# The last token tile of a Conformer kernel: residual on TensorE, two halves of the features, statistics and normalisation from PSUM on two engines, square root on ScalarE

## Chip, cores, metric

One core of one Trainium2 chip. The metric is the device time of one execution in microseconds, median of several. The kernel before takes 2054.47 us (median of 3 runs, 2052.74 to 2055.17), so a tail of a few microseconds is all that this change can touch.

## The reference

A Conformer block in bf16: x is 2 x 4000 tokens of 512 features. The last step is what matters here: half of the second feed-forward's result is added to x3, and the sum is normalised over the 512 features of each token.

```python
def _layernorm(x, axis=-1, eps=1e-05):
    m = jnp.mean(x, axis=axis, keepdims=True)
    v = jnp.var(x, axis=axis, keepdims=True)
    return (x - m) / jnp.sqrt(v + eps)
...
    h = _layernorm(x3, axis=-1)
    h = _silu(h @ w_ff2_a) @ w_ff2_b        # 512 -> 2048 -> 512
    x4 = x3 + 0.5 * h
    return _layernorm(x4, axis=-1)
```

## The kernel before

Tokens are worked in chunks of four tiles of 127 tokens; the last chunk has three. `ff_last` is the second feed-forward of that last chunk and the last work of the kernel. For each tile it accumulates 16 matmuls of 512 columns in one PSUM bank, then VectorE adds the residual, takes mean and variance, GpSimd takes the power -1/2, VectorE normalises, and two queues (SP 112 rows, ACT 15 rows) store.

```python
    def ff_last(self, c, old):
        ...                                        # 16 blocks of the first matmul and Silu
        sl = self.nxt("ln", self.LN_SLOTS)
        for ti in range(token_tiles(c)):
            for f in range(FC):
                self.ff_second(f, ti, *blocks[f], f == FC - 1)
            self.residual(self.Yb[ti][0:TILE, :], self.b_Y[ti], c * TPC + ti, 0.5)
            self.ln_stats(c, sl, ti)               # DVE bn_stats from SBUF
            self.ln_mean(sl, ti)                   # DVE bn_aggr
            self.ln_factor(sl, ti)                 # DVE add eps, POOL pow -0.5
            self.ln_norm(c, sl, ti, self.osb[0][:, ti, :], self.b_osb[0][ti], "DVE")
            self.store_out(c, self.osb[0], self.b_osb[0], ti, ti + 1, ("SP", "ACT"))

    def residual(self, ps, b_ps, g, scalar, b_scalar=(), rows=slice(0, TILE)):
        self.S.op("DVE", lambda e: e.scalar_tensor_tensor(
            out=self.XT[g][rows], in0=ps[rows], scalar=scalar, in1=self.XT[g][rows], op0=ALU.mult, op1=ALU.add),
            reads=[b_ps, self.bx[g]] + list(b_scalar), writes=[self.bx[g]])
```

Two other places come into the argument. The program ends with a branch that every engine takes past a second program (a fallback that this input does not need), and the place where the attention loop starts pieces of the convolution:

```python
    def build(self):
        ...
        self.program(False)
        fits = nc.values_load(self.flag, ...)
        self.wait_out()
        with nc.If(fits < 1):                      # the fallback program
            S.barrier()
            self.program(True)
            self.wait_out()
...
        def att_hook(g, kt):
            ...
            if kt in (22, 27) and (0 <= g - 1 < tail or g - 1 == tail and (22, 27).index(kt) < self.KEEP):
                pair(g - 1, (22, 27).index(kt))    # matmuls on tiles that the SP queue transposes
```

## Time and profile before

| | kernel before |
|---|---|
| time, median of 3 | 2054.47 us |
| span of the profiled run, granted clock | 2047.4 us, 1.000 |
| first matmul of the last tile to the store's issue on SP | 6.63 us |
| of which after the last matmul's end | 3.01 us |
| store's issue to its last landing; to the end of the span | 2.44; 2.63 us |

The last three rows are read from the timeline of the last 10 us and from the store's landings; the prediction below shows the timeline's lines. "Landing" is the moment at which the store's completion reaches the semaphore that SP waits for before it ends; in this profile that is 0.91 us after the packet of the last row has ended (1.52 us after the issue).

The view of the store's own instructions of the kernel before, cut to the last one, gives the landings of its two queues (us from issue):

```profile
DMA to landing us min/median/max: 1.9/2.2/2.4
```

The 15 rows of the ACT queue land after 1.9 us, the 112 rows of SP after 2.4.

### The profile page before, as it was taken

The numbers are of one execution on the slowest core, as the hardware profiler recorded it, in microseconds if no ns is written. First come the engines' busy times: TensorE is split into PE (matmuls) and PEld (weight loads), VectorE is DVE, ScalarE is ACT, GpSimd is POOL, SyncE is SP. The second block draws the span as 40 slices with busy tenths as digits, with TensorE's granted clock in tenths as the row PEclk, the third lists the DMA queues.
The fourth block names the chain that finished last, engine by engine and source line by source line (L and its number), as shares of the span: only waits on it lengthen the run. The fifth ranks groups of instructions, "written<-read, shape, count | busy, mean of one in ns | idle before, by whom it ended". The sixth has DMA issues, their size and how long they took to land.

```text
span 2047.4 us, 24513 instructions
## 1 busy us (share of the span) xinstructions
PE 2029.9 (99%) x9647; PEld 1028.7 (50%) x9649; DVE 1092.7 (53%) x2264; ACT 744.9 (36%) x1274; POOL 109.7 (5%) x236
## 2 busy tenths in 40 slices
PE   9999999999999999999999999999999999999998
PEld 5555555554444444444444444444445555555555
DVE  4244443334556667666766676667674434434434
ACT  3433333333333333333333333333345443433433
POOL 1000000000000000000000000000011000000000
PEclk9999999999999999999999999999999999999999
DMA  8222245420101011104411111011143111111111
GB/s 182 54 62 62 53 100 125 96 70 8 26 16 31 22 31 26 30 24 108 113 34 23 26 29 32 23 26 29 42 135 93 31 31 42 31 31 42 26 36 38
DMA packets 253120, 104.41 MB, mean 51 GB/s; under 512 B 193412, under 2 KB 252487, under 8 KB 252999
## 3 DMA queue, kind: packets, MB, share of 16 engines
q1 hardware_dynamic: 252751, 102.61, 21.2%
q8 instruction: 78, 1.28, 0.3%
q14 instruction: 43, 0.35, 0.1%
q10 hardware_dynamic: 248, 0.18, 0.0%
HBM read 33.77 MB, written 23.34 MB: 28 GB/s over the span
## 4 chain that ended last, share of the span: by engine, by line
PE 97%; DVE 1%; DMA 0%; SPq 0%; issue 0%; POOL 0%; ACT 0%; POOLq 0%; DVEq 0%; ACTq 0%
PE s L500 55%; PE y L500 42%; DVE wff L1176 0%; SPq L558 0%; DVE work L612 0%; DMA work<-work 0%; DMA wff<-in_w_ff_a_dram 0%; DVE xt L753 0%; SPq L562 0%; DVE work L634 0%; POOL work L726 0%; POOL work L1185 0%; ACT work L550 0%; DVE work L547 0%; SPq L554 0%
## 5 line engine op out<-in xcount | busy, mean ns | idle before, releaser
L550 ACT ACTIVATE work<-s 128x508 bf16<-128x508 f32 (+3 forms) x1060 | 622.8, 588 | 1211.9 <-PE s L500 1208.3
L500 PE MATMUL s<-work,wff 128*128 128x508 bf16 (+5 forms) x2624 | 628.3, 371 | 6.4 <-issue 3.5
L500 PE MATMUL s<-work,keys 128*128 128x508 bf16 (+1 forms) x2048 | 516.8, 374 | 0.1
L500 PE MATMUL y<-work,keys 128*128 128x508 bf16 (+2 forms) x2048 | 504.2, 373 | 0.4 <-DVE work L999 0.4
L500 PE MATMUL y<-wff,work 128*127 128x512 bf16 x1992 | 501.2, 379 | 0.0
L920 DVE TENSOR_TENSOR work<-work 128x508 f32<-128x508 f32 (+2 forms) x496 | 334.5, 674 | 279.8 <-ACT work L550 278.6
L500 PEld LDWEIGHTS s<-work,wff 128*128 128x128 bf16 x2624 | 252.2, 98 | 283.1 <-issue 10.1
L500 PEld LDWEIGHTS y<-wff,work 128*127 128x127 bf16 x1992 | 273.7, 137 | 171.4
L500 PEld LDWEIGHTS s<-work,keys 128*128 128x128 bf16 x2048 | 199.5, 98 | 231.9 <-issue 0.6
L500 PEld LDWEIGHTS y<-work,keys 128*128 128x128 bf16 (+1 forms) x2048 | 193.5, 97 | 234.0 <-issue 6.2
L753 DVE SCALAR_TENSOR_TENSOR xt<-y,xt 127x512 bf16<-127x512 f32 x126 | 78.5, 683 | 360.5 <-PE y L500 360.5
L612 DVE BATCH_NORM_STATS2 work<-xt 127x6 f32<-127x512 bf16 x312 | 197.2, 680 | 5.9 <-DMA xt<-in_x_dram 5.8
L500 PE MATMUL s<-work 128*127 128x512 bf16 (+3 forms) x776 | 197.0, 378 | 2.2 <-DVE work L1292 1.2
L621 POOL TENSOR_TENSOR work<-work 127x4 f32<-127x4 f32 (+1 forms) x76 | 76.7, 1009 | 1133.6 <-DVE work L619 1133.6
L500 PEld LDWEIGHTS s<-work 128*127 128x127 bf16 (+1 forms) x776 | 94.9, 124 | 77.0 <-issue 3.8
L634 DVE TENSOR_SCALAR work<-xt,work 127x512 bf16<-127x512 bf16 x307 | 110.7, 406 | 26.2 <-POOL work L621 23.0
L753 DVE SCALAR_TENSOR_TENSOR xt<-s,xt 127x512 bf16<-127x512 f32 x55 | 38.0, 692 | 144.6 <-PE s L500 144.6
L753 DVE SCALAR_TENSOR_TENSOR xt<-s,work,xt 127x512 bf16<-127x512 f32 x64 | 48.0, 750 | 30.8 <-PE s L500 30.2
L1074 DVE SCALAR_TENSOR_TENSOR wff<-wff,s 128x508 bf16<-128x508 f32 (+1 forms) x57 | 38.7, 678 | 45.3 <-PE s L500 45.1
L550 ACT ACTIVATE wff<-s 128x508 f32<-128x508 f32 (+1 forms) x67 | 39.5, 591 | 58.7 <-PE s L500 58.7
L550 ACT ACTIVATE work<-keys,work 128x508 bf16<-128x508 bf16 (+1 forms) x68 | 52.2, 774 | 1.4 <-DVE work L1190 1.3
L1155 POOL COPY wff<-wff 128x1 bf16<-128x1 bf16 x56 | 10.5, 188 | 638.8 <-DVE wff L1074 636.4
(83 smaller groups left out, 424.0 us busy)
## 6 DMA issues: line engine op xcount, KB each, us to landing
keys<-keysd SPq DMA_DIRECT2D x62, 128.0 KB, 2.3
keysd<-work SPq DMA_DIRECT2D x14, 448.0 KB, 3.2
out_dram<-work SPq DMA_DIRECT2D x14, 448.0 KB, 3.2
dcvd<-wff SPq DMA_DIRECT2D x48, 127.0 KB, 1.8
keys<-dcvd SPq DMA_DIRECT2D x12, 508.0 KB, 5.1
xt<-in_x_dram SPq DMA_DIRECT2D x13, 448.0 KB, 4.9
wff<-in_w_ff_a_dram SPq DMA_DIRECT2D x16, 256.0 KB, 6.3
work<-work SPq DMA_TRANSPOSE x208, 2.5
```

What stands on the lines that cost most here:

```text
L500: self.S.op("PE", lambda e: e.matmul(out, lhsT, rhs, start=start, stop=stop, **kw), reads=reads, writes=[bank], inc=stop if inc is None el ...
L550: return self.S.op("ACT", lambda e: e.activation(out, in_, func, **kw), reads=reads, writes=writes)
L612: self.S.op("DVE", lambda e: e.bn_stats(self.st[sl][:, ti, :], x), reads=[b_x], writes=[self.b_st[sl][ti]])
L621: S.op("POOL", lambda e: e.tensor_tensor(out=self.rs[sl][:, 0:n], in0=self.va[sl][:, 0:n], in1=self.neghalf[0:TILE, 0:n], op=ALU.pow), rea ...
L634: self.S.op("DVE", lambda e: e.tensor_scalar(out, x, self.mv[sl][:, ti, 0:1], self.rs[sl][:, ti:ti + 1], ALU.subtract, ALU.mult), reads=[b ...
L753: self.S.op("DVE", lambda e: e.scalar_tensor_tensor(out=self.XT[g][rows], in0=ps[rows], scalar=scalar, in1=self.XT[g][rows], op0=ALU.mult, ...
L920: S.op("DVE", lambda e, p=p, n=n, acc=acc: e.tensor_tensor(out=acc, in0=acc, in1=self.P[p][0:n, 0:W], op=ALU.add), reads=[self.b_P[p], sel ...
L1074: self.S.op("DVE", lambda e: e.scalar_tensor_tensor(out=out, in0=th, scalar=1.0, in1=ps[:, 0:W], op0=ALU.add, op1=ALU.mult), reads=[b_ps, ...
L1155: S.op("POOL", lambda e: e.tensor_copy(self.G[gs][:, jj, 0:1], self.G[gp][:, jj, CHUNK:CHUNK + 1]), reads=[self.b_G[gp][jj]], writes=[self ...
```

## The change

The intent: shorten the chain behind the last matmul. TensorE, which accumulates anyway, adds 2·x through a matmul with twice the identity (so PSUM holds 2·x3 + h; a layernorm of twice the vector with four times epsilon is the same); the features go in two halves to two banks, so that the first half's statistics run beside the second half's matmuls; the factor comes from ScalarE's square root and a reciprocal; and VectorE and ScalarE normalise one half each straight from PSUM. Setup lines and declarations are cut.

```diff
@@ def ff_last(self, c, old):
+        S.op("DVE", lambda e: e.tensor_scalar(self.two, self.ident, 2.0, None, ALU.mult), ...)
...
-        sl = self.nxt("ln", self.LN_SLOTS)
-        for ti in range(token_tiles(c)):
+        self.act(self.nr1, self.onef, AF.Sqrt, [self.b_onef], [self.b_nr1])     # loads the table early
+        sl, n = self.nxt("ln", self.LN_SLOTS), token_tiles(c)
+        for ti in range(n - 1):
...
+        ti, g = n - 1, c * TPC + n - 1
+        st, b_st = self.st[sl][:, ti:ti + 2, :], self.b_st[sl][ti:ti + 2]
+        halves = [(self.Yb[k], self.b_Y[k], slice(m * D // 2, (m + 1) * D // 2)) for m, k in enumerate((0, ti))]
+        for m, (ps, b_ps, d) in enumerate(halves):
+            self.mm(ps[0:TILE, d], self.two[0:TILE, 0:TILE], self.XT[g][:, d], True, False, [self.b_two, self.bx[g]], b_ps)
+            for f, (p, b_p) in enumerate(blocks):
+                self.mm(ps[0:TILE, d], p[:, ti * TILE:(ti + 1) * TILE], self.Wb[:, f, d], False, f == FC - 1,
+                        [self.b_Wb[f], b_p], b_ps)
+            S.op("DVE", lambda e, m=m, ps=ps, d=d: e.bn_stats(st[:, m, :], ps[0:TILE, d]), reads=[b_ps], writes=[b_st[m]])
+        S.op("DVE", lambda e: e.bn_aggr(self.mv[sl][:, ti, :], st.rearrange("p t s -> p (t s)")), ...)
+        self.act(sd, self.mv[sl][:, ti, 1:2], AF.Sqrt, [...], [b_sd], bias=self.eps4[0:TILE])     # 4 * EPS
+        S.op("DVE", lambda e: e.reciprocal(self.rs[sl][:, ti:ti + 1], sd), ...)
+        S.op("DVE", lambda e: e.scalar_tensor_tensor(out=sh, in0=mean, scalar=-1.0, in1=rs, op0=ALU.mult, op1=ALU.mult), ...)
+        for m, (ps, b_ps, d) in enumerate(halves):
+            if m == 0:
+                S.op("DVE", lambda e, ps=ps, d=d: e.tensor_scalar(o[:, d], ps[0:TILE, d], mean, rs, ALU.subtract, ALU.mult), ...)
+            else:
+                self.act(o[:, d], ps[0:TILE, d], AF.Identity, [...], [b_o[ti + 1]], bias=sh, scale=rs)
+        self.store_out(c, self.osb[0], b_o, ti, ti + 2, ("SP", "ACT"))
```

More of the change, by code (lines that the diff above doesn't have):

```diff
@@ L384, in memory @@
         self.b_late = [A.buf("late", k * 1024, 2 * CHUNK) for k in range(FC - self.NP)]
+        self.two = A.view(60 * 1024, 128)
+        self.b_two = A.buf("two", 60 * 1024, 256)
         ns = self.LN_SLOTS
@@ L412, in memory @@
         self.b_nr1 = Buf("nr1")
+        self.eps4 = small(1)
+        self.b_eps4 = Buf("eps4")
         self.onef = small(1)
@@ L795, in ff_last @@
         S, late = self.S, FC - self.NP
+        S.op("DVE", lambda e: e.tensor_scalar(self.two, self.ident, 2.0, None, ALU.mult), reads=[self.b_ident], writes=[self.b_two])
         blocks = []
@@ L817, in ff_last @@
             self.store_out(c, self.osb[0], self.b_osb[0], ti, ti + 1, ("SP", "ACT"))
+        ti, g = n - 1, c * TPC + n - 1
[7 more added lines that the diff above has]
+            S.op("DVE", lambda e, m=m, ps=ps, d=d: e.bn_stats(st[:, m, :], ps[0:TILE, d]), reads=[b_ps], writes=[b_st[m]])
+        S.op("DVE", lambda e: e.bn_aggr(self.mv[sl][:, ti, :], st.rearrange("p t s -> p (t s)")),
+             reads=b_st, writes=[self.b_mv[sl][ti]])
+        sd, b_sd = self.va[sl][:, ti:ti + 1], self.b_va[sl][ti]
+        self.act(sd, self.mv[sl][:, ti, 1:2], AF.Sqrt, [self.b_mv[sl][ti], self.b_eps4], [b_sd], bias=self.eps4[0:TILE])
+        S.op("DVE", lambda e: e.reciprocal(self.rs[sl][:, ti:ti + 1], sd), reads=[b_sd], writes=[self.b_rs[sl][ti]])
+        o, b_o = self.osb[0][:, ti, :], self.b_osb[0]
+        mean, rs, sh = self.mv[sl][:, ti, 0:1], self.rs[sl][:, ti:ti + 1], self.sh[sl][:, ti:ti + 1]
+        b_mv, b_rs, b_sh = self.b_mv[sl][ti], self.b_rs[sl][ti], self.b_sh[sl][ti]
+        S.op("DVE", lambda e: e.scalar_tensor_tensor(out=sh, in0=mean, scalar=-1.0, in1=rs, op0=ALU.mult, op1=ALU.mult),
+             reads=[b_mv, b_rs], writes=[b_sh])
+        for m, (ps, b_ps, d) in enumerate(halves):
+            if m == 0:
+                S.op("DVE", lambda e, ps=ps, d=d: e.tensor_scalar(o[:, d], ps[0:TILE, d], mean, rs, ALU.subtract, ALU.mult),
+                     reads=[b_ps, b_mv, b_rs], writes=[b_o[ti]])
+            else:
+                self.act(o[:, d], ps[0:TILE, d], AF.Identity, [b_ps, b_sh, b_rs], [b_o[ti + 1]], bias=sh, scale=rs)
+        self.store_out(c, self.osb[0], b_o, ti, ti + 2, ("SP", "ACT"))
     def store_out(self, c, o, b_o, lo, hi, engs=("SP",)):
@@ L1296, in constants @@
         S.op("POOL", lambda e: e.memset(self.onef, 1.0), writes=[self.b_onef])
+        S.op("POOL", lambda e: e.memset(self.eps4, 4 * EPS), writes=[self.b_eps4])
         S.op("DVE", lambda e: e.memset(self.XT[SHARED][HALF - 32:HALF], 0.0), writes=[self.bx[SHARED]])
```

## The prediction

> **What bounds the kernel now.** I read the page first. The busy line says how full TensorE is, and the chain of work that ended last says who sets the end.
>
> ```profile
> PE 2029.9 (99%) x9647; PEld 1028.7 (50%) x9649; DVE 1092.7 (53%) x2264; ACT 744.9 (36%) x1274; POOL 109.7 (5%) x236
> PE 97%; DVE 1%; DMA 0%; SPq 0%; issue 0%; POOL 0%; ACT 0%; POOLq 0%; DVEq 0%; ACTq 0%
> ```
>
> TensorE is the bound for 97% of a span of 2047.4 us, and the change does not touch that part. It can only act where TensorE has nothing left to do, so I next read the timeline from the last matmul on (start us, length us, engine, line, operation, shapes, count).
>
> ```profile
> 2041.35 0.38 PE L500 MATMUL y<-wff,work 128*127 128x512 bf16 x1
> 2041.77 0.69 DVE L753 SCALAR_TENSOR_TENSOR xt<-y,xt 127x512 bf16<-127x512 f32 x1 [0.54 <-PE y L500]
> 2042.49 0.69 DVE L612 BATCH_NORM_STATS2 work<-xt 127x6 f32<-127x512 bf16 x1
> 2043.22 0.18 DVE L719 BATCH_NORM_AGGREGATE work<-work 127x2 f32<-127x6 f32 x1
> 2043.44 0.15 DVE L724 TENSOR_SCALAR work<-work 127x1 f32<-127x1 f32 x1
> 2043.67 0.55 POOL L726 TENSOR_TENSOR work<-work 127x1 f32<-127x1 f32 x1 [2.89 <-DVE work L724]
> 2044.25 0.41 DVE L634 TENSOR_SCALAR work<-xt,work 127x512 bf16<-127x512 bf16 x1 [0.66 <-POOL work L726]
> 2044.74 0.32 SPq L822 DMA_DIRECT2D out_dram<-work  x1
> 2044.75 0.37 ACTq L822 DMA_DIRECT2D out_dram<-work  x1
> ```
>
> This is a chain with one link at a time: each row starts 0.03 to 0.05 us after the one above ends, and only one engine works. The matmuls end at 2041.73, the last row of results is ready at 2044.66, the store is issued at 2044.74, and the span ends at 2047.4. So the exposed tail is 5.7 us: 3.0 us of compute and hand-offs, and 2.65 us of store with the final waits. The change can shorten the first part only; the store still moves 112 and 15 rows over the same two queues. A ceiling follows: even if the whole 3.0 us vanished, that is 0.15% of the time. A verdict outside 2% is out of reach.
>
> Rows of other parts of the same trace price the new pieces: a stretch of the chain, two stretches of the timeline, and the groups by shape (busy us, mean ns of one).
>
> ```profile
> 2031.37 6.92 PE y L500 x32
> ...
> 11.91 1.91 PE L500 MATMUL s<-work,wff 128*128 128x254 bf16 x16 [0.61 <-DVE work L547]
> ...
> 1520.29 0.74 PE L500 MATMUL s<-work 128*127 128x1 bf16 x8
> ```
>
> ```profile
> L1183 DVE BATCH_NORM_AGGREGATE work<-wff 128x2 f32<-128x21 f32 x3 | 0.7, 249 | 0.1
> ...
> L992 DVE RECIPROCAL work<-work 127x4 f32<-127x4 f32 x15 | 2.7, 180 | 0.5
> ...
> L634 DVE TENSOR_SCALAR work<-s,work 127x512 bf16<-127x512 f32 x2 | 1.5, 804 | 0.3 <-POOL work L726 0.3
> ...
> L1190 DVE SCALAR_TENSOR_TENSOR work<-work 128x1 f32<-128x1 f32 x4 | 0.6, 154 | 1.5 <-POOL work L1185 1.5
> ...
> L550 ACT ACT_TABLE_LOAD x4 | 5.1, 1283 | 2.0 <-issue 1.9
> ...
> L550 ACT ACTIVATE work<-s,work 127x512 bf16<-127x512 f32 x2 | 1.4, 768 | 0.0
> ...
> L550 ACT ACTIVATE work<-work 128x1 f32<-128x1 f32 x3 | 0.6, 203 | 0.0
> ```
>
> **What the Trainium skill says.** (1) "TensorE: Matmul & The Clock Gate", section "Back-to-back issue gap": an isolated matmul of N columns follows the one before after N / 2.4 + 2.5 ns. The trace agrees: 6.92 us / 32 = 216 ns at N = 512, and (1.91 - 0.27) / 15 = 109 ns at N = 254 (0.27 us being the last one's own length). (2) The same page, "Weight-path perf modes", says that the fast weight load needs 128 weights. This tile has 127, and the trace agrees that such loads are longer (137 against 98 ns mean). Whether that binds with half the columns per load is a question below. (3) "ScalarE: Activation LUTs", "Table sets: the hidden batching unit", has cheap functions such as identity in every table set, and square root in a set of its own; "What ACT_TABLE_LOAD costs" gives 1283 ns, which the four loads of this trace match, and about 93 ns more for each per-partition operand. The trace agrees with the latter: Identity from PSUM with two such operands takes 768 ns, a plain copy of that shape 597. (4) "VectorE: DVE Perf Modes", "Why PSUM operands drop a tier": a PSUM source loses the fast modes. Agreed: the normalisation takes 804 ns from PSUM and 406 from SBUF.
>
> **The change, part by part.** All times are on the clock of the timeline above; only the third tile of the last chunk changes.
>
> *TensorE.* Before: 16 matmuls of 512 columns. After: two passes of 1 + 16 matmuls of 256 columns, the extra one of each being twice the identity by x. The third tile's first matmul starts at 2041.35 - 15 x 0.216 = 2038.11. The 34th starts 33 x 0.109 = 3.60 later, at 2041.71, and takes 0.27: end 2041.98, **0.26 later** than before. The first half is complete at about 2040.13. Its statistics wait behind tile two's normalisation on VectorE (ends 2041.23) and run to about 2041.7: hidden.
>
> *Removed from the chain:* the residual, 0.69 plus a hand-off of 0.03: **-0.73**.
>
> *Statistics.* 512 elements from PSUM take about 0.69; half of them, at about 1.05 ns each (508 and 444 elements take 688 and 619 ns), take 0.69 - 0.27 = 0.43: **-0.26**. The two halves go to different banks, so no engine reads where TensorE writes.
>
> *Aggregate.* 6 elements take 0.18 and 21 take 0.25, so 12 take about 0.21: **+0.03**.
>
> *The factor.* Before: from the end of the aggregate (2043.40) to the start of the normalisation (2044.25), 0.85 us: add epsilon 0.15, power on GpSimd 0.55, three hand-offs. After: hand-off 0.04, square root on ScalarE 0.30 (0.203 for one element and 0.09 for the bias operand), hand-off 0.04, reciprocal 0.16 (0.18 for four elements), 0.03, the shift -mean x factor 0.16, hand-off 0.04: ScalarE's half starts 0.77 after the aggregate: **-0.08**. So the square root is hardly better than the power; the gain is mostly in the parts above.
>
> *The normalisation.* Before: 0.41 from SBUF in bf16. After: ScalarE's 256 columns from PSUM take 0.768 less 256 columns at 0.83 ns (that page's rate; copies of 508 and 381 columns, 594 and 491 ns, give 0.81) = 0.555, and VectorE's take 0.804 - 0.27 = 0.54. VectorE needs no shift and follows it at once, so it ends some 0.13 earlier and ScalarE sets the end: 0.555 against 0.41: **+0.14**. Halving the columns on two engines is thus no gain at all: a whole tile from SBUF was already cheaper than half a tile from PSUM.
>
> *Off the path:* the table load for the square root (1.28) falls after the last Silu, at about 2031.9, when ScalarE has nothing to do until its store issue at 2037.96; one VectorE operation for the doubled identity, where VectorE is idle; one memset at the start. The store waits for two engines instead of one, with both waits at hand: +0.0.
>
> Sum: +0.26 - 0.73 - 0.26 + 0.03 - 0.08 + 0.14 = **-0.64 us**. The store is then issued at about 2044.10 instead of 2044.74, and the span is about 2046.8 us. The time: 2054.47 - 0.64, about **2053.8 us**.
>
> **The rivals.** (a) *Weight loads bind the short matmuls.* The number of loads doubles, and if one 137 ns load had to pass per matmul, 34 would take 4.66 us and TensorE would end 1.2 later instead of 0.26: time about 2054.8, slower than before. For it: the 137 ns row. Against it: the eight one-column matmuls with 127-column loads fill 0.74 us; less the last one's 0.2 that is under 80 ns each, with a start-up wait in it. A load's period is well below 109 ns, so it should hide. I give it 12%.
> (b) *A table load between square root and Identity*, if the tables do not share Identity: +1.28 on the path, time about 2055.1. Against it: four loads in the whole trace although Silu, Copy and Identity alternate near the start. 4%.
> (c) *The hand-offs eat the gain.* The chain now goes VectorE, ScalarE, VectorE, ScalarE, and the store has two releasers. With each of the five crossings 0.1 instead of 0.04, 0.3 is lost: time 2054.1. Some of it is plausible.
> (d) *The gain is larger*, if the square root's bias costs nothing extra and the last Identity is shorter: about -0.9, time 2053.6.
>
> All of them lie within 0.05% of the time before, under the spread of its own three runs (2052.74 to 2055.17), and the profiled run of before took 2051.23. So the **range** is noise, not mechanism: a median that holds -0.64 and moves by about 2 us between sessions gives 2051.5 to 2055.4 us. Chances: faster by over 2%, 0.005; within 2%, 0.985; slower by over 2%, 0.01 (an unforeseen stall or a slow run).
>
> **What would show it.** In the profile after, the timeline of the tail should have: 34 matmuls of 256 columns at 109 ns and an end at about 2041.98 (rival a: 2042.9); first-half statistics ended before the last matmul; then statistics 0.43, aggregate 0.21, square root 0.30, reciprocal 0.16, shift 0.16, and the last Identity 0.55, starting before VectorE's half ends; no GpSimd row in the tail; a fifth table load near 2032 and none after (rival b); store issue 2.1 us after the last matmul's end instead of 3.0. Rival (c) shows as gaps over 0.06 between these rows. What would make the prediction wrong is a change of more than 1 us in the part before 2038, which the change should leave alone, or a store that takes as much longer as it is issued earlier.

## The result, and the profile after

| | before, same rounds | changed |
|---|---|---|
| time, median of 4 runs | 2053.88 us (2052.74 to 2055.17) | 2053.41 us (2052.68 to 2054.72) |
| profiled run: time, span, clock | 2051.23, 2047.4, 1.000 | 2054.14, 2050.1, 0.998 |

A ratio here is the mean time of one kernel's fast runs over the mean of the other's fast runs of the same rounds, so it is not quite the ratio of the medians. It is 0.9998, with a 95% interval of 0.9981 to 1.0016: the same.

The changed kernel's page, busy line and chain of what ended last:

```profile
PE 2032.7 (99%) x9667; PEld 1031.0 (50%) x9667; DVE 1092.8 (53%) x2266; ACT 746.2 (36%) x1278; POOL 108.9 (5%) x236
...
PE 97%; DVE 1%; DMA 0%; SPq 0%; issue 0%; POOL 0%; ACT 0%; DVEq 0%; ACTq 0%
```

Two things are already odd. TensorE is busy 2.8 us longer (2032.7 against 2029.9), where the change costs it 0.3; and the profiled span is 2.7 us longer although the change shortens something. So look at the tail first. Timeline of the changed kernel, from the last tile's first matmul (start, length, engine, line, operation, shapes, count, and the idle time before it):

```profile
2041.00 0.27 PE L505 MATMUL y<-xt,keys 127*127 127x256 bf16 x1
...
2042.86 0.27 PE L505 MATMUL y<-xt,keys 127*127 127x256 bf16 x1
...
2043.85 1.04 PE L505 MATMUL y<-wff,work 128*127 128x256 bf16 x8
2044.03 0.42 DVE L835 BATCH_NORM_STATS2 work<-y 127x6 f32<-127x256 f32 x1
2044.92 0.43 DVE L835 BATCH_NORM_STATS2 work<-y 127x6 f32<-127x256 f32 x1 [0.47 <-PE y L505]
2045.39 0.21 DVE L836 BATCH_NORM_AGGREGATE work<-work 127x2 f32<-127x12 f32 x1
2045.63 0.29 ACT L555 ACTIVATE work<-work 127x1 f32<-127x1 f32 x1 [9.34 <-DVE work L836]
2045.96 0.16 DVE L840 RECIPROCAL work<-work 127x1 f32<-127x1 f32 x1 [0.36 <-ACT work L555]
2046.16 0.16 DVE L844 SCALAR_TENSOR_TENSOR work<-work 127x1 f32<-127x1 f32 x1
2046.24 0.54 DVE L848 TENSOR_SCALAR work<-y,work 127x256 bf16<-127x256 f32 x1
2046.35 0.56 ACT L555 ACTIVATE work<-y,work 127x256 bf16<-127x256 f32 x1 [0.42 <-DVE work L844]
2046.99 0.37 ACTq L857 DMA_DIRECT2D out_dram<-work  x1
```

The tail starts at 2041.00 instead of 2038.11: **2.9 us are lost before the change begins to act.** Inside, the tail is as designed. The first half's statistics (2044.03 to 2044.45) run beside the second half's matmuls, the square root takes 0.29, the halves are normalised side by side, and SP issues at 2046.98. From the first matmul to the issue it is 5.977 us; it was 6.627. So **0.65 us are gained, where 0.64 was predicted.**

Behind the issue, the same view of the store as before:

```profile
DMA to landing us min/median/max: 2.7/2.8/2.9
```

The store of the same 127 rows takes 0.5 us longer. Of the 0.65 gained, 0.18 is left at the end of the span (9.085 us from the tail's first matmul to the end, against 9.261). That leaves two questions: what happened before 2041, and why is the last store slower?

### The profile page after: what moved, and what is told of

Same layout as the page of the kernel before. It is cut to its first block, busy times and chain, and to the rows that moved or that the text cites. A ratio compares the mean times of both kernels' runs of the same rounds, so it can differ in the third digit from the quotient of the medians.

```text
span 2050.1 us, 24557 instructions
## 1 busy us (share of the span) xinstructions
PE 2032.7 (99%) x9667; PEld 1031.0 (50%) x9667; DVE 1092.8 (53%) x2266; ACT 746.2 (36%) x1278; POOL 108.9 (5%) x236
## 3 DMA queue, kind: packets, MB, share of 16 engines
q8 instruction: 78, 1.28, 0.3%
## 4 chain that ended last, share of the span: by engine, by line
PE 97%; DVE 1%; DMA 0%; SPq 0%; issue 0%; POOL 0%; ACT 0%; DVEq 0%; ACTq 0%
PE s L505 55%; PE y L505 42%; DVE wff L1211 0%; DMA work<-work 0%; SPq L563 0%; DVE work L617 0%; DMA wff<-in_w_ff_a_dram 0%; ACT work L555 0%; SPq L567 0%; POOL work L1220 0%; DVE xt L758 0%; DVE work L955 0%; DVE work L639 0%; DVE work L552 0%; POOL work L731 0%
## 5 line engine op out<-in xcount | busy, mean ns | idle before, releaser
L505 PE MATMUL y<-wff,work 128*127 128x512 bf16 (+1 forms) x2000 | 501.4, 378 | 0.0
```

The costliest lines, as they stand in the source:

```text
L505: self.S.op("PE", lambda e: e.matmul(out, lhsT, rhs, start=start, stop=stop, **kw), reads=reads, writes=[bank], inc=stop if inc is None el ...
```

## The experiments

Twelve kernels ran, four per call on the same chip (each call on another one); each gave the reference's result. In what follows "tail" is the stretch from the last tile's first matmul to the store's issue on SP, and "flight" the time from issue to the last landing.

### Are both effects real? The two kernels again

The edit: none. *b_again* is the kernel before, *a_again* the changed one.

> The kernel before, unchanged, against itself: the noise floor. Ratio 1.000, interval about 0.1% wide on each side, which would hide the 0.03% of the tail. The profile gives a second sample of three things that the change cannot touch: the flight of the last store (2.45 us in the first profile of before, 2.93 in that of after), the wait of TensorE near 963 us (start to start of the two matmuls around it: 3.85 and 5.07 us), and whether the half clock follows that wait. If the half clock is a matter of luck and not of the change, some runs of this kernel too have a mean clock of 0.998. Tail, from the first matmul of the last tile to the issue of the last store: 6.63 us again, to within 0.03.

> The changed kernel, unchanged. Tail, from the first matmul of the last tile to the issue of the last store: 5.98 us again, to within 0.03 (0.65 less than before). Ratio of times 0.9997 if only the tail counts, not to be told from 1. If the longer store flight of the first profile (2.93 us) belongs to the change (two producers, two halves), it is near 2.9 again here and near 2.45 in all runs of the kernel before; if it is chance, both kernels show both values.

Measured: *b_again* 2053.3 us (2050.38 to 2055.12, ratio to the kernel before 0.9997, 0.9983 to 1.0010); *a_again* 2054.03 us (2053.09 to 2054.81, ratio 1.0000, 0.9987 to 1.0014). The tails repeat to 3 ns: 6.628 and 5.980. The flight of before repeats as well (2.448), but that of the changed kernel is now 3.774 us. The store's view of *a_again*:

```profile
DMA to landing us min/median/max: 3.6/3.7/3.8
```

What follows: the slow flight belongs to the changed kernel, and its size varies. Here it takes all that the tail gained and 0.7 us more (9.950 us from first matmul to end, against 9.272).

The time before the tail, on the other hand, does not belong to the change. *b_again*'s tail starts at 2040.52, nearly as late as the changed kernel's 2041.00. The timeline of TensorE near 960 us shows it. First the kernel before, then the changed one, both in their first profiles:

```profile
962.56 0.91 PE L500 MATMUL y<-work,keys 128*128 128x444 bf16 x4
966.97 1.89 PE L500 MATMUL s<-work,wff 128*128 128x508 bf16 x8 [3.50 <-issue]
```

```profile
961.91 0.91 PE L505 MATMUL y<-work,keys 128*128 128x444 bf16 x4
967.54 3.54 PE L505 MATMUL s<-work,wff 128*128 128x508 bf16 x8 [4.71 <-issue]
```

In both, eight matmuls of the convolution start late. The profile names no releaser ("issue"); I take it that they wait for transposes that stand on the SP queue behind reloads of keys, and the next experiment tests that. In the changed kernel's profile the wait is 4.7 us, and then the same eight matmuls take 3.54 instead of 1.89 us: half the clock. The windows view of that profile (window, length, busy PE, PEld, DVE, ACT, POOL with counts, granted clock, DMA share, GB/s) confirms it:

```profile
965.40:972.30 6.90, 4.76 (x12) 1.77 (x13) 0.69 (x1) 0.59 (x1) 0.30 (x2) 0.51 0.53 127
```

The trace's clock records give the half-clock stretch as 6.827 us in that profile, 3.413 in *b_again*'s and none in the first profile of before. The stretch begins at 965.40, still in the wait, so TensorE works in only some 4.7 us of it (4.76 busy in the view) and loses half of that, about 2.35. With a wait that is 1.22 us longer (962.56 to 966.97 against 961.91 to 967.54) and the 0.65 us by which this profile was ahead before it, that is the 2.9 us before the tail; 2.35 and the change's own 0.3 are most of the 2.8 us more of busy time. Runs of the unchanged kernel show the reduced mean clock too (0.998 in most), so it is a disturbance of both kernels, and a comparison of two single profiles puts it down to the change by mistake.

### Taking the disturbance away: *b_shift* and *a_shift*

In both kernels, the two convolution pieces of one chunk are started four and three key steps later, when their transposes have come.

```diff
-            if kt in (22, 27) and (0 <= g - 1 < tail or g - 1 == tail and (22, 27).index(kt) < self.KEEP):
-                pair(g - 1, (22, 27).index(kt))
+            kts = (26, 30) if g == TCB - 1 else (22, 27)
+            if kt in kts and (0 <= g - 1 < tail or g - 1 == tail and kts.index(kt) < self.KEEP):
+                pair(g - 1, kts.index(kt))
```

> The kernel before with one edit in the middle: in the query chunk whose key reloads fill the SP queue, the two convolution blocks are asked for at key steps 26 and 30 instead of 22 and 27, four steps of 1.5 us later, so that their transposed input has landed. Theory: TensorE's wait near 963 us (3.85 to 5.07 us) disappears, and with it the half clock of 6.8 us that cost 3.5 us more in the first profile of after. Expected: no start-to-start distance over 0.5 us near 963, mean clock 1.000 in all runs, time lower by 4 us where the half clock did not fall and by 8 where it did: 2045 to 2049 us, ratio 0.996 to 0.998. Rival: the queue is short of time altogether, so that the wait moves to a later step and the time stays.

> The changed kernel with the same edit in the middle. With the wait and the half clock gone from both, the runs should scatter less and the tail's 0.65 us should show as a difference of the medians between this and the kernel before with the edit: 0.3 to 1.0 us. If the changed tail were worth nothing in time (given back in the store), the two medians would agree to 0.2 us.

Measured: *b_shift* 2050.02 us (2049.94 to 2051.74), ratio 0.9983 (0.9969 to 0.9997); *a_shift* 2051.51 us (2051.2 to 2051.81), ratio 0.9990 (0.9976 to 1.0003). That misses what was expected for *b_shift* (2045 to 2049 us), and *a_shift* is not 0.3 to 1.0 us below *b_shift* but 1.5 us above it. The wait near 963 us and the half clock behind it are gone; the windows view of *b_shift* has TensorE busy for all of 12 us at full clock:

```profile
960.00:972.00 12.00, 12.00 (x64) 6.06 (x63) 5.19 (x9) 3.83 (x7) 0.00 (x0) 1.00 0.64 116
```

Smaller waits come instead near 1001 and 1013 us (1.0 to 2.3 us from one matmul's start to the next), none with half a clock behind it, in all seven profiles with this edit. So the rival was right in part: the two waits together are 2.9 to 4.1 us, where the single one was 3.9 to 5.1, and what goes is above all the half clock. In the seven profiles without the edit it follows the length of the wait: none after 3.85 us, 3.41 us of it after 4.07 and 4.33, 6.83 us after 4.57 to 5.07. Some 2.5 to 3.4 us are won between the medians, in either kernel. The tails are untouched (6.630 and 5.981), and so is the question: the flight is 2.676 in *b_shift* and 3.595 in *a_shift*. So the slow store has nothing to do with what happens mid-kernel.

### Why is the store slower? Moving TensorE's last instruction fetch

What differs in the store's window is one line of the DMA view. First the kernel before, then *a_shift2* (the changed kernel with the shift; below), each in the window from 0.75 us after its store's issue to just before the end of its span (queue, packets, MB, share of 16 engines):

```profile
q1 hardware_dynamic: 128, 0.11, 23.4%
q10 hardware_dynamic: 30, 0.02, 3.4%
q14 instruction: 2, 0.02, 2.5%
```

```profile
q1 hardware_dynamic: 128, 0.11, 12.4%
q8 instruction: 1, 0.02, 3.3%
q14 instruction: 3, 0.02, 2.1%
q10 hardware_dynamic: 30, 0.02, 1.7%
```

The store's rows go on q1 and q10. In the second there is a packet on **q8**, an instruction fetch. The trace's own records say that it is 16,384 bytes and takes 0.88 to 1.81 us; 78 of them come in a run, 1.28 MB, about 66 bytes for each of the 19.3 thousand matmuls and weight loads. From that I take q8 for TensorE's instruction stream. The Trainium skill, "Runtime: NRT & Kernel Launch", section "Instruction fetch mechanics", says that a sequencer refills its instruction memory in blocks of 16 KiB by its own DMA queue, that crossing a block is mostly hidden, and that a taken branch breaks the sequential prefetch. The trace agrees with the size on q8 (q14, the queue of the other instruction packets, moves 8,192 bytes at a time); whether the cost is hidden is what is tested here.

The explanation, called R: TensorE's sequencer runs ahead of the array, and when it has handed out its last matmul it takes the branch at the end of the program, after which two more blocks are fetched (for what, the trace does not show). In the kernel before, the branch begins 6.49 us before the store's issue, 3.48 us before the last matmul's end; in the changed kernel 3.65 us before the issue, 1.56 us before that end. 3.48 us are 16 matmuls of 216 ns, 1.56 us are 14 of 109 ns: the lead is a number of instructions, so with matmuls of half the length it is about half as long. With the tail shorter as well, the second fetch slips from before the store into the store.

The rival: the store is slow for another reason (two engines write its rows, it is issued sooner after the store of the tile before, the fetches of other engines), and q8 stands beside it by chance.

The test moves the branch alone. Matmuls into a PSUM bank that nobody reads follow the last tile; they do not touch the tail, but keep TensorE's sequencer busy.

```diff
         self.store_out(...)
+        p, b_p = blocks[0]
+        for k in range(N):                     # 13 in b_pad13, 18 in a_pad18
+            self.mm(self.Sb[0][0:TILE, :], p[:, 0:TILE], self.Wb[:, 0, :], True, True, [self.b_Wb[0], b_p], self.b_S[0], inc=k == N - 1)
```

*b_pad13* gives the kernel before (with the shift) the changed kernel's branch time; *a_pad18* gives the changed kernel (with the shift) a branch so late that its second fetch comes after the store. *b_shift2* and *a_shift2* are *b_shift* and *a_shift* again, for the same rounds.

> The changed kernel with the edit in the middle, and 18 dummy matmuls of 512 columns after the last real one (into an idle bank, results unused), so that TensorE's own end, its branch and the instruction fetches that follow come later. Theory R (refill): the last store is late in the changed kernel because a 16 KB instruction fetch of TensorE, which starts 4.1 to 5.1 us after its branch begins, falls into the time in which the store's packets move (+0.8 to +2.0 us after issue). The branch begins some 16 matmuls before the end of its stream: 3.65 us before the store's issue in the changed kernel. With the dummies it should begin about 1.7 us before, so that one fetch lies before the packets and the next after them. Expected: store flight 2.1 to 2.5 us instead of 2.9 to 3.8, tail to the issue unchanged (2.09 us from the last real matmul's end), time lower than the changed kernel with the edit alone by about 1.2 us, although TensorE has more to do. Rival W (two producers): the flight is long because the rows come from two engines; then it stays at 2.9 to 3.8. Rival L (program end): TensorE's later end delays the whole; then the time rises by 2 us.

> The reverse test: the kernel before with the edit in the middle, its old tail untouched, and 13 dummy matmuls after the last real one, so that TensorE's branch begins about 3.65 us before the store's issue as in the changed kernel, not 6.49. Theory R: the second fetch now falls on the store, flight 2.9 to 3.8 us instead of 2.2 to 2.45, and the time rises by 0.5 to 1.4 us over the kernel before with the edit. Rival W: nothing changes, flight 2.2 to 2.5.

> The kernel before with the edit in the middle again, as the base of this call: median near 2050.0 us, flight 2.2 to 2.5 us, no half clock in the middle.

> The changed kernel with the edit in the middle again: flight 2.9 to 3.8 us, median 1 to 1.6 us above that of the kernel before with the same edit if the first call was no accident; if it was, 0.6 us below.

Measured, from the trace's records, all in us after the store's issue on SP; the last column is from the tail's first matmul to the end of the span:

| profile | tail | branch starts | second q8 fetch | flight | first matmul to end |
|---|---|---|---|---|---|
| before | 6.627 | -6.49 | -1.98 to -1.04 | 2.44 | 9.26 |
| b_again | 6.628 | -6.49 | -1.98 to -0.99 | 2.45 | 9.27 |
| b_shift | 6.630 | -6.49 | -2.02 to -1.08 | 2.68 | 9.44 |
| b_shift2 | 6.626 | -6.49 | -1.16 to -0.22 | 2.55 | 9.37 |
| **b_pad13** | 6.629 | -3.68 | +1.57 to +2.58 | **3.57** | 10.33 |
| after | 5.977 | -3.65 | +0.46 to +1.55 | 2.91 | 9.09 |
| a_again | 5.980 | -3.66 | +1.45 to +2.42 | 3.77 | 9.95 |
| a_shift | 5.981 | -3.66 | +0.67 to +2.25 | 3.60 | 9.77 |
| a_shift2 | 5.976 | -3.65 | +1.14 to +2.95 | 4.10 | 10.27 |
| **a_pad18** | 5.977 | -1.52 | +2.92 to +3.95 | **2.88** | 8.99 |

The store's view of *b_pad13*, with the q8 line of its DMA view (from 0.75 us after the issue), and then the store's view of *a_pad18*:

```profile
DMA to landing us min/median/max: 2.8/3.2/3.6
```

```profile
q8 instruction: 1, 0.02, 2.2%
```

```profile
DMA to landing us min/median/max: 2.6/2.8/2.9
```

The kernel before becomes slow to store (3.57 against 2.44 to 2.68) although nothing of its tail or store has changed. The changed kernel falls to 2.88: below the 3.60 to 4.10 of its last three profiles, but not below the 2.91 of its first, and not to the 2.1 to 2.5 that was expected. Taken alone, this flight does not decide; *b_pad13* and the packets do.

Where the fetch ends late, the store lands 1.0 to 1.4 us after the fetch's end: 1.55 and 2.91, 2.42 and 3.77, 2.25 and 3.60, 2.95 and 4.10, 2.58 and 3.57. The packets show how. An undisturbed store has started all its 127 rows by 1.47 to 1.50 us after the issue. In *a_again*, *a_shift* and *a_shift2* exactly eight rows start only when the fetch has ended (in *a_again* from 2.404, the fetch ending at 2.418): 127 rows over 16 DMA engines are eight for each, so this is the share of the one DMA engine that the fetch holds. In *b_pad13* the fetch starts at 1.57, when 126 rows have started (by 1.51); the last one, of the ACT queue, starts at 2.54, and the 3.57 is the landing of that queue (SP's 112 rows landed at 2.76). The Trainium skill, "DMA: Bandwidth & Descriptors", section "Queues, rings and completion order", says that a DMA engine serves its queues in turn and finishes a whole packet of one before the next. The rows behave in that way towards the 16 KB record; whether it is one packet in that page's sense (a group of descriptors) the trace does not show.

R stands, and the rival falls: neither two writers nor the earlier issue is in *b_pad13*. The other engines' fetches don't explain it either: q14's packets stand at 0.52 to 0.83 and 1.60 to 1.91 us there, at 0.60 to 0.95 and 1.56 to 1.86 in the kernel before. Nor does the padding as such: *a_pad18* has more of it and a shorter flight.

But q14 can do the same in other runs, and this is enough to account for what *a_pad18* keeps above the kernel before (0.2 to 0.4 us). There a q14 packet of 8,192 bytes moves from 0.81 to 1.49 us after the issue, and eight rows follow one another from 1.487 on, the last at 2.08. In the changed kernel's first profile a q14 packet (1.20 to 1.51) and the q8 packet hold eight rows each. What stays open is why the same branch's second fetch ends anywhere from 1.55 to 2.95 us after the issue. Each padded kernel has one profile.

The times cannot show this. *a_pad18* 2050.85 us (2050.14 to 2051.58, ratio 0.9986, 0.9972 to 1.0000), *b_pad13* 2051.2 (2050.59 to 2052.18, 0.9988, 0.9975 to 1.0002), *b_shift2* 2050.75 (2050.02 to 2053.34, 0.9990, 0.9977 to 1.0004), *a_shift2* 2050.74 (2049.34 to 2052.03, 0.9986, 0.9972 to 0.9999): all four equal within their spread, so neither the 1.2 us that *a_pad18* should have saved (it is 0.1 above *a_shift2*) nor the 0.5 to 1.4 us that *b_pad13* should have cost (it is 0.45 above *b_shift2*) can be told. *a_shift* was 1.5 us above *b_shift* and *a_shift2* equals *b_shift2* here, so neither difference of medians is to be explained. The conclusion rests on the profiles.

### Which part gains what: *res_alone*, *halves_alone*, *a_pow*

*res_alone* is the kernel before with the residual on TensorE alone: one bank, 1 + 16 matmuls of 512 columns, then VectorE and GpSimd as before, reading PSUM.

```diff
-            self.residual(...)                 # last tile only
+        self.mm(ps[0:TILE, :], self.two[0:TILE, 0:TILE], self.XT[g], True, False, [self.b_two, self.bx[g]], b_ps)
+        ...                                    # 16 matmuls of 512 columns, start=False
+        self.ln_factor(sl, ti, 4 * EPS)        # the rest as before, from PSUM
```

*halves_alone* has the two banks of 256 columns, with residual and statistics for each half on VectorE, power and normalisation as before.

```diff
+        for m, (ps, b_ps, d) in enumerate(halves):
+            ...                                # 16 matmuls of 256 columns
+            x = self.XT[g][:, d]
+            S.op("DVE", ... e.scalar_tensor_tensor(out=x, in0=ps[0:TILE, d], scalar=0.5, in1=x, ...))
+            S.op("DVE", ... e.bn_stats(st[:, m, :], x))
```

*a_pow* is the changed kernel with the factor as before.

```diff
-        self.act(sd, self.mv[sl][:, ti, 1:2], AF.Sqrt, ..., bias=self.eps4[0:TILE])
-        S.op("DVE", lambda e: e.reciprocal(self.rs[sl][:, ti:ti + 1], sd), ...)
+        S.op("DVE", lambda e: e.tensor_scalar(sd, self.mv[sl][:, ti, 1:2], 4 * EPS, None, ALU.add), ...)
+        S.op("POOL", lambda e: e.tensor_tensor(out=self.rs[sl][:, ti:ti + 1], in0=sd, in1=self.neghalf[...], op=ALU.pow), ...)
```

> The residual by TensorE alone: one bank of 512 columns, 1 + 16 matmuls, statistics and normalisation of the whole tile from PSUM on VectorE, factor by GpSimd as before. From the first matmul of the last tile to the store's issue before took 6.63 us. Expected: one matmul more (+0.22), no residual (-0.73), the normalisation from PSUM (0.80 instead of 0.41: +0.39): 6.51 us, so this part alone is worth 0.12. Theory R on the store: the branch begins 16 matmuls of 216 ns ahead, some 6.2 us before the issue, and the fetch ends before the packets move: last landing 2.4 to 2.7 us after the issue.

> The two halves alone: 32 matmuls of 256 columns into two banks, but the residual on VectorE in halves, statistics in halves from SBUF, factor by GpSimd and normalisation from SBUF as before. VectorE is busy with tile two until 3.1 us after the first matmul, and then has four half operations of 0.43 us in a row: they end at 4.86, the aggregate at 5.10, factor 0.85, normalisation 0.41: issue at 6.44 us, so this part alone is worth 0.19 and the last matmul's end does not set the time. Together with the one before the two are worth more than their sum. Theory R: branch about 4.3 us before the issue, the fetch at about -0.2 to +2: partly on the packets, last landing 2.4 to 3.6 us.

> The changed kernel with GpSimd's power (add of epsilon on VectorE, then power) in the place of the square root and the reciprocal; the rest unchanged. The factor is ready 0.86 us after the aggregate instead of 0.56: tail to the issue 6.28 instead of 5.98 us, +0.30. If the square root were no better than the power, as in a reading that leaves out the shift which this form needs behind the factor, it would stay at 5.98 to 6.05. Theory R: branch 3.95 us before the issue, fetch on the packets: last landing 2.9 to 4.1 us.

Measured, one run each (2052.44, 2054.15 and 2055.05 us, which says nothing at this spread), from the traces:

| | tail | against 6.627 | branch starts | second q8 fetch | flight | first matmul to end |
|---|---|---|---|---|---|---|
| res_alone | 6.528 | -0.10 | -6.17 | -1.56 to -0.61 | 2.46 | 9.19 |
| halves_alone | 6.415 | -0.21 | -4.32 | -0.19 to +1.14 | 2.46 | 9.07 |
| a_pow | 6.267 | -0.36 | -3.94 | +0.18 to +1.30 | 2.77 | 9.23 |
| changed kernel | 5.977 | -0.65 | -3.65 | see above | 2.91 to 4.10 | 9.09 to 10.27 |

The three parts that were measured singly (0.10, 0.21, and the square root's 0.29 below, by taking it out) make 0.60 of the 0.65; the rest goes with combining them and with the normalisation on two engines, which was not run alone. The residual on TensorE saves a VectorE operation but costs an extra matmul and makes statistics and normalisation read all 512 columns from PSUM. Halves alone are limited by VectorE, which still has tile two to finish and then four operations of 0.42 to 0.43 us. The square root, which the prediction called hardly better than the power, is worth 0.29 us **here**: with add and power the factor takes 0.85 us without a shift, and with the 0.19 of the shift that ScalarE's half needs 1.04; with the square root it is 0.754, shift included. The flights agree with R once more: only with matmuls of 256 columns does the branch come late. In *halves_alone* and *a_pow* the fetch ended early (1.14 and 1.30), and the last rows started at 1.71 and 1.96 us, not long after the 1.48 of the kernel before; so the flight suffered little or nothing, less in *a_pow* than expected (2.77 against 2.9 to 4.1). I count these two as agreeing, not as a test.

### A version that keeps the gain: *best_pad16*

The changed kernel with the shift, halves of 304 and 208 columns (the second half's statistics and normalisation are on the path, the first's are not), ScalarE's Abs_reciprocal_sqrt in place of square root and reciprocal, and 16 unread matmuls at the end that move the fetch behind the store.

```diff
-        halves = [... slice(m * D // 2, (m + 1) * D // 2) ...]
+        halves = [(self.Yb[0], self.b_Y[0], slice(0, 304)), (self.Yb[ti], self.b_Y[ti], slice(304, D))]
-        self.act(sd, ..., AF.Sqrt, ...)
-        S.op("DVE", lambda e: e.reciprocal(self.rs[sl][:, ti:ti + 1], sd), ...)
+        self.act(self.rs[sl][:, ti:ti + 1], self.mv[sl][:, ti, 1:2], AF.Abs_reciprocal_sqrt, [...], [...], bias=self.eps4[0:TILE])
```

> A version meant to beat both: the changed kernel with the edit in the middle, 16 dummy matmuls at the end, columns split 304 to 208 (VectorE starts its part 0.12 us before ScalarE), and one ScalarE function for the inverse square root in place of square root and reciprocal (its accuracy is not known here; the comparison with the reference decides). Tail to the issue: 5.98 less 0.20 (no reciprocal and hand-off) less 0.05 to 0.09 (shorter second half): 5.70 us. Theory R: branch about 1.8 us before the issue, fetches before and after the packets, last landing 2.4 to 2.9 us. Time 2049.5 to 2050.5 us, ratio to the kernel before 0.9982 to 0.9988.

Measured: 2050.11 us (2049.06 to 2050.2), ratio 0.9981 (0.9967 to 0.9994), and the result is correct. The timeline of its tail:

```profile
2040.20 0.38 DVE L835 BATCH_NORM_STATS2 work<-y 127x6 f32<-127x208 f32 x1 [0.42 <-PE y L505]
2040.61 0.21 DVE L836 BATCH_NORM_AGGREGATE work<-work 127x2 f32<-127x12 f32 x1
2040.86 0.29 ACT L555 ACTIVATE work<-work 127x1 f32<-127x1 f32 x1 [9.29 <-DVE work L836]
2041.18 0.16 DVE L843 SCALAR_TENSOR_TENSOR work<-work 127x1 f32<-127x1 f32 x1 [0.36 <-ACT work L555]
2041.44 0.52 ACT L555 ACTIVATE work<-y,work 127x208 bf16<-127x208 f32 x1 [0.29 <-DVE work L843]
```

The reciprocal is gone from the chain and the last statistics are 0.05 shorter; the tail is 5.751 us (0.05 over what was expected), the second fetch comes 3.05 us after the issue, the flight is 2.86, and the end comes 8.80 us after the first matmul against 9.26 to 9.44 before. That half microsecond is seen in the profile alone. In the times nearly all of its 0.19% is the shift, which by itself brought the kernel before to 2050.0 and 2050.8. A variant with the power on VectorE in place of GpSimd's did not compile.

## Why the prediction was right, and where it was not

**The time** was right, 2053.41 us against 2053.8, but for a reason that the prediction itself gave: everything in play is smaller than the spread of the runs. It is no proof of the mechanism.

**The compute tail** was right term by term:

| term | predicted | measured |
|---|---|---|
| last matmul's end, 34 matmuls 109.4 ns apart | +0.26 | +0.27 |
| residual | -0.73 | -0.73 |
| statistics (0.693 to 0.434) | -0.26 | -0.26 |
| aggregate (0.182 to 0.208) | +0.03 | +0.03 |
| factor, aggregate's end to the normalisation (0.851 to 0.754) | -0.08 | -0.10 |
| normalisation (0.412 to 0.563) | +0.14 | +0.15 |
| hand-off to the store (0.075 to 0.062) | 0.0 | -0.01 |
| sum | -0.64 | -0.65 |

One reading of the old chain was too short: the prediction has every row start 0.03 to 0.05 us after the one above, but by its own lines two links take 0.08, from VectorE to GpSimd (2043.59 to 2043.67) and from the normalisation to the store (2044.66 to 2044.74). The sum used the measured 0.85 for the first, and the second stays nearly as it was (0.062), so nothing was lost by it. And "the square root is hardly better than the power" holds against the old form only: in the new one, which needs the shift, it is worth 0.29 us (*a_pow*).

**Rivals (a) to (d)**: (a) weight loads do not bind, as the matmuls keep their 109 ns; (b) the fifth table load falls at 2034.80, off the path, and none follows; (c) the hand-offs are 0.03 to 0.04; (d) the gain is not larger. None of the four came.

**The step that failed** is "The store waits for two engines instead of one, with both waits at hand: +0.0", and with it "The change can shorten the first part only". The store's issue did cost nothing more, but the 2.65 us behind it were taken for a constant. From the issue to the end of the span it is 2.71 us on average over four profiles of before (2.63 to 2.81; two plain, two with the shift) and 3.79 over the same four of the changed kernel (3.11 to 4.29): **+1.08, not 0.0**. So the true sum is -0.65 + 1.08 = +0.43 us: from the tail's first matmul to the end, the changed kernel is on average slower (9.77 against 9.34), and only in its first profile a little faster. The gain was given back by TensorE's own instruction fetch (in the first profile together with one of q14), which no rival named. The prediction's last sentence named the symptom, "a store that takes as much longer as it is issued earlier", without a cause.

**Also failed**: that nothing changes before 2038. The first profile after had 2.9 us there, which is the mid-kernel wait with its half clock that the kernel before has too. It was not an effect of the change, and *b_again* was needed to see it.

## What to carry to other kernels

When a change shortens the chain before the last store, check the store's flight from issue to landing, too: what the other engines do as they finish (here an instruction fetch for a branch) can collide with it, and a shorter tail or shorter matmuls bring that forward or back. Before a difference of a few microseconds between two profiles is put down to a change, profile the unchanged kernel again: here its tail began 2.4 us later in the second profile than in the first. And what a part is worth depends on the chain that it stands in: the square root was reckoned at 0.08 us against the old chain and is worth 0.29 in the new one.

## What the Trainium skill lacked or had wrong

- "Runtime: NRT & Kernel Launch", section "Instruction fetch mechanics", calls the cost of crossing an instruction block mostly hidden, and for a branch tells of a stall of the engine that fetches. It lacks what the fetch costs others: here a 16 KB fetch after the closing branch took 0.97 to 1.81 us and held up to eight rows of the last store, and the flight grew from 2.44 to as much as 4.10 us; 8 KB fetches on q14 held eight rows too.
- No page that I read says how far TensorE's closing branch precedes the array's end: 3.48 us with matmuls of 512 columns, 1.56 with 256, so about a fixed number (14 to 16) of matmuls.
- "TensorE: Matmul & The Clock Gate", section "Back-to-back issue gap", gives a sustained 131 ns per matmul of 512 columns with weight loads. Here such pairs ran at 216 ns (6.92 us for 32), the formula for the isolated one; at 256 columns and 127 weights at 109.4 ns.
- The same page, section "LDWEIGHTS (loading the stationary operand)", gives P / 1.2 ns, 106 ns for 127 columns. Here one such load took longer (137 ns mean), but between matmuls of one column loads of 127 columns followed one another every 59 ns (at 1520 us in the kernel before), so neither figure is a limit for the rate.
